# One level of Strassen's algorithm in the first product of a four-expert mixture layer

## The chip, the cores and the metric

The kernel runs on one core of one Trainium2 chip. The metric is the device time of one execution in microseconds (us). TensorE (PE) multiplies, VectorE (DVE), ScalarE (ACT) and GpSimd (POOL) work element by element, and SyncE (SP) issues the transfers. Each engine takes its instructions in the order in which the program lists them, and semaphores order the engines among each other.

## What is computed

```python
# attention on q, k, v in chunks of 64 tokens -> x [2304, 512]
a = x @ w_a; b = x @ w_b                  # [512, 1536] each
x = (a * b) @ w_out                       # [1536, 512]
p = domain_probs / (domain_probs.sum(-1, keepdims=True) + 1e-09)
for e in range(4):                        # w1 [4, 512, 1024], w2 [4, 1024, 512]
    h = np.maximum(x @ w1[e], 0.0)
    out += p[:, e:e + 1] * (h @ w2[e])
```

The change concerns the products `x @ w1[e]` and the order of everything in the loop over the experts.

## The kernel before

The 2304 tokens are 18 tiles of 128, in five blocks: block 0 has two tiles (256 tokens), blocks 1 to 4 have four (512 tokens). Activations lie with the features on the partitions and the tokens along the free dimension until the last product.

Every dense product is taken on float32r parts. An operand is split as hi, its rounding to float32r (a cast on ACT, `split_hi`, L84), and lo, the remainder (a subtraction, on POOL for the weights, L158). `mm3` (L305 to L312) issues three matmuls for each 128 rows of the contraction: hi·lo, hi·hi, lo·hi. Each matmul has its own weight load.

The first stage runs attention beside the first of 12 chunks of `w_a`, `w_b`, `w_out` (`moe1_steps`, `x2_steps`). For each chunk and block: the a products (12 matmuls), the b products (12), a copy of a on ACT (L336), the product a·b on DVE (L340), its split (hi on ACT, lo on POOL, L344); and one block later the 12 matmuls with `w_out`, whose results DVE adds to `xacc` (L374). In the last chunk each finished quarter of `xacc` is split on the spot into `yh` (ACT) and `yl` (POOL, L377): those are the inputs of the mixture.

The second stage (L523 to L532) walks 16 groups g of two chunks of 128 hidden features, and in each the five blocks. `emit_h` makes one chunk's hidden values of a block: 12 matmuls into one PSUM bank, `hh` by Relu on ACT (L392), `hl` by DVE from the same bank (L393). `emit_o`, one block behind, makes for each tile the 6 matmuls with w2 and one DVE instruction (L423) that scales by p and adds to `oacc`; the last group also stores. Two blocks' work is interleaved this way so that the hidden values are ready when their products come:

```python
for j in range(NB):
    for f in range(g * G2, g * G2 + G2):
        emit_h(f, j)
    if pend:
        emit_o(*pend)
    pend = (g, j)
```

Weights come in pieces of [128, 512] through three `raw` buffers (`load_w`, on SP, L109); a piece is loaded when the piece three before it has been split. Six `wh`/`wl` pairs hold the split pieces. PSUM is used as a ring of eight banks (`psum`, L75). The order of instructions on every engine is the order of the source (`manual_schedule`); the semaphores follow from the tiles.

Of the kernel before, what the change touches and what calls it, by code (L numbers as in the profile page):

```python
# [28 lines left out]
def fused_kernel(  # L29
# [104 lines left out]

    ready = {}

    def prep_begin(n, upto):
        for _ in range(n):
            if nxt["begin"] < min(upto, len(pieces)):
                key = pieces[nxt["begin"]]  # L140
                nxt["begin"] += 1
                r = raws.pop(key)
                ready[key] = from_f64(r) if key[0] == 0 else r

    def prep_end(n, upto):
        for _ in range(n):
            if nxt["prep"] < min(upto, len(pieces)):
# [3 lines left out]
                if key[0] == 1 and nxt["prep"] % 4 == 0:  # L151
                    pool, n_b = late["h"], 2
                else:
                    pool, n_b = w_p, 6
                hi = pool.tile([P, 512], F32R, tag="wh", name="wh", bufs=n_b)
                lo = pool.tile([P, 512], F32R, tag="wl", name="wl", bufs=n_b)
                split_hi(hi, r)
                nc.gpsimd.tensor_tensor(out=lo, in0=r, in1=hi.bitcast(F32), op=ALU.subtract)  # L158
                wts[key] = (hi, lo)
# [226 lines left out]
    def emit_h(f, j):
        n = blocks[j][1] * P
        ps = psum()
        mm3(ps, kparts(wts[1, f, 0], xh[j], xl[j]), n)
        hh = late["h"].tile([P, 512], F32R, tag="hh", name="hh", bufs=2 * G2)  # L390
        hl = late["h"].tile([P, 512], F32R, tag="hl", name="hl", bufs=2 * G2)
# [202 lines left out]
```

## Time and profile before

| | us |
|---|---|
| median of 3 runs (lowest, highest) | 1311.74 (1311.53, 1312.3) |
| span of the profiled execution | 1309.5 |
| busy in that span: PE, DVE, POOL, ACT | 1296.1, 619.2, 291.9, 279.8 |

The busy time of PE counts a matmul from its start to its end, and successive matmuls overlap, so a matmul's own duration is not what one more matmul costs; that is the distance from one start to the next. The second stage, from 519.4 us on, takes some 60% of the span.

### The profile page before, as it was taken

Reading aid. Unit: us, or ns where it says so; the run is one execution under the profiler, and the core shown is the slowest. Engines: PE = TensorE matmul, PEld = TensorE weight load, DVE = VectorE, ACT = ScalarE, POOL = GpSimd, SP = SyncE. Lnnn points to the kernel's source line nnn. Section 1 sums busy time; section 2 is a strip of 40 time slices with the busy share of each in tenths; the row PEclk is TensorE's granted clock in tenths of the full one; section 3 lists DMA queues with packets and bytes.
Section 4 is the critical chain, followed back from the end, with each engine's and each line's share of the span. In section 5 each row is a group of like instructions: output and inputs, shape, how many; then the busy total and the mean of one; then the engine's idle time right before and its main releaser. Section 6 shows DMA issues by size and latency. Waiting matters only on the chain.

```text
span 1309.5 us, 16332 instructions
## 1 busy us (share of the span) xinstructions
PE 1296.1 (99%) x6818; PEld 1083.4 (83%) x6820; DVE 619.2 (47%) x985; ACT 279.8 (21%) x517; POOL 291.9 (22%) x247
## 2 busy tenths in 40 slices
PE   8899999999999999999999999999999999999998
PEld 5788888888888888888888888888888888888887
DVE  7964555555655544344344344344344344344344
ACT  3544222222222225111111111111111111111110
POOL 4523333433433338210110110110110110110100
PEclk9999999999999999999999999999999999999999
DMA  8721111111111000100000000000000000000003
GB/s 273 221 89 33 40 41 35 47 49 49 49 37 45 25 25 25 33 20 22 25 18 23 25 19 23 25 18 24 25 18 23 25 18 24 25 17 24 1 24 121
DMA packets 25272, 55.60 MB, mean 42 GB/s; under 512 B 3184, under 2 KB 3184, under 8 KB 25200
## 3 DMA queue, kind: packets, MB, share of 16 engines
q1 hardware_dynamic: 25200, 54.58, 13.5%
q8 instruction: 53, 0.87, 0.3%
q14 instruction: 19, 0.16, 0.0%
HBM read 49.84 MB, written 4.72 MB: 42 GB/s over the span
## 4 chain that ended last, share of the span: by engine, by line
PE 94%; DVE 4%; issue 0%; ACT 0%; DMA 0%; POOL 0%; SPq 0%; DVEq 0%
PE ps L310 31%; PE ps L311 31%; PE ps L312 31%; PE ps L261 1%; DVE d L212 1%; DVE sm L223 0%; DVE mx L210 0%; DVE cv L116 0%; PE ps L196 0%; DVE xl L274 0%; DVE sm L224 0%; DMA kbd<-in_k_dram 0%; DVE cv L119 0%; DVE cv L122 0%; PE ps L233 0%
## 5 line engine op out<-in xcount | busy, mean ns | idle before, releaser
L423 DVE SCALAR_TENSOR_TENSOR oacc<-ps,pr,oacc 128x512 f32<-128x512 f32 x270 | 202.8, 751 | 129.4 <-PE ps L312 127.0
L393 DVE SCALAR_TENSOR_TENSOR hl<-ps,hh 128x512 fp32r<-128x512 f32 (+1 forms) x160 | 102.1, 638 | 329.9 <-ACT hh L392 329.9
L311 PE MATMUL ps<-yh,wh 128*128 128x512 f32 (+1 forms) x640 | 235.4, 368 | 0.0
L312 PE MATMUL ps<-yh,wl 128*128 128x512 f32 (+1 forms) x640 | 235.4, 368 | 0.0
L310 PE MATMUL ps<-yl,wh 128*128 128x512 f32 (+1 forms) x640 | 235.3, 368 | 0.0
L392 ACT ACTIVATE hh<-ps 128x512 fp32r<-128x512 f32 (+1 forms) x160 | 88.8, 555 | 655.2 <-PE ps L312 655.1
L310 PE MATMUL ps<-wl,hh 128*128 128x512 f32 x576 | 224.3, 389 | 0.0
L311 PE MATMUL ps<-wh,hh 128*128 128x512 f32 x576 | 224.2, 389 | 0.0
L312 PE MATMUL ps<-wh,hl 128*128 128x512 f32 x576 | 224.1, 389 | 0.0
L158 POOL TENSOR_TENSOR wl<-raw,wh 128x512 fp32r<-128x512 f32 x64 | 82.7, 1292 | 633.4 <-ACT wh L84 633.4
L310 PE MATMUL ps<-xl,wh 128*128 128x512 f32 (+1 forms) x488 | 179.7, 368 | 3.4 <-DVE xl L274 2.9
L311 PE MATMUL ps<-xh,wh 128*128 128x512 f32 (+1 forms) x488 | 178.1, 365 | 0.0
L312 PE MATMUL ps<-xh,wl 128*128 128x512 f32 (+1 forms) x488 | 178.0, 365 | 0.0
L310 PEld LDWEIGHTS ps<-yl,wh 128*128 128x128 f32 x640 | 120.6, 188 | 20.5
L311 PEld LDWEIGHTS ps<-yh,wh 128*128 128x128 f32 x640 | 120.6, 188 | 20.5
L312 PEld LDWEIGHTS ps<-yh,wl 128*128 128x128 f32 x640 | 120.6, 188 | 20.0
L374 DVE TENSOR_TENSOR xacc<-ps,xacc 128x512 f32<-128x512 f32 (+1 forms) x220 | 132.7, 634 | 2.4 <-PE ps L312 2.4
L340 DVE TENSOR_TENSOR asb<-ps,asb 128x512 f32<-128x512 f32 (+1 forms) x61 | 38.5, 630 | 197.0 <-PE ps L312 170.4
L312 PEld LDWEIGHTS ps<-wh,hl 128*128 128x128 f32 x576 | 108.1, 188 | 22.6
L310 PEld LDWEIGHTS ps<-wl,hh 128*128 128x128 f32 x576 | 108.2, 188 | 22.1
L311 PEld LDWEIGHTS ps<-wh,hh 128*128 128x128 f32 x576 | 108.2, 188 | 21.9
L344 POOL TENSOR_TENSOR gl<-asb,gh 128x512 fp32r<-128x512 f32 (+1 forms) x61 | 71.5, 1172 | 168.5 <-ACT gh L84 168.5
(55 smaller groups left out, 1297.5 us busy)
## 6 DMA issues: line engine op xcount, KB each, us to landing
raw<-in_w1p_dram SPq DMA_DIRECT2D x36, 512.0 KB, 3.5
raw<-in_w2p_dram SPq DMA_DIRECT2D x64, 256.0 KB, 2.6
q<-in_q_dram SPq DMA_DIRECT2D x18, 256.0 KB, 4.7
kbd<-in_k_dram SPq DMA_DIRECT2D x36, 128.0 KB, 4.5
v<-in_v_dram SPq DMA_DIRECT2D x18, 256.0 KB, 3.5
out_dram<-oacc SPq DMA_DIRECT2D x18, 256.0 KB, 2.0
pr<-in_probs_dram SPq DMA_DIRECT2D x1, 36.0 KB, 4.3
```

The costliest lines, as they stand in the source:

```text
L158: nc.gpsimd.tensor_tensor(out=lo, in0=r, in1=hi.bitcast(F32), op=ALU.subtract)
L212: nc.vector.tensor_tensor(out=d, in0=ps, in1=mx.to_broadcast([P, H, CH]), op=ALU.subtract)
L261: nc.tensor.matmul(out=ps[s, hp, CH * c : CH * c + CH], lhsT=vv[s, c, hp, :], rhs=aT[s, hp, CH * c : CH * c + CH], start=True, stop=True,)
L310: nc.tensor.matmul(out=ps[:, :n], lhsT=wh, rhs=al, start=(m == 0), stop=False)
L311: nc.tensor.matmul(out=ps[:, :n], lhsT=wh, rhs=ah, start=False, stop=False)
L312: nc.tensor.matmul(out=ps[:, :n], lhsT=wl, rhs=ah, start=False, stop=(m == last))
L340: nc.vector.tensor_tensor(out=g[:, :n], in0=st[1][:, :n], in1=g[:, :n], op=ALU.mult)
L344: nc.gpsimd.tensor_tensor(out=gl[:, :n], in0=g[:, :n], in1=gh[:, :n].bitcast(F32), op=ALU.subtract)
L374: nc.vector.tensor_tensor(out=ac, in0=ps[:, :n], in1=ac, op=ALU.add)
L392: nc.scalar.activation(out=hh[:, :n], in_=ps[:, :n], func=ACTF.Relu)
L393: nc.vector.scalar_tensor_tensor(out=hl[:, :n], in0=ps[:, :n], scalar=0.0, in1=hh[:, :n].bitcast(F32), op0=ALU.max, op1=ALU.subtract,)
L423: nc.vector.scalar_tensor_tensor(out=o, in0=ps, scalar=p1, in1=o, op0=ALU.mult, op1=ALU.add)
```

## The change

The hidden values of blocks 1 and 2, and of 3 and 4, are made in pairs. For a group g, w1 is a 2×2 matrix of blocks (features in halves of 256, hidden chunks two) and the two token blocks with the feature halves are another. Instead of eight block products, `emit_h_pair` takes seven, each of 6 matmuls (`half_mm`), in Winograd's form of Strassen's algorithm: of sums S1 to S4 of w1's quarters and sums T1 to T4 of the activations' quarters. The results are put together by DVE additions through three temporary tiles (`u2`, `u3`, `c22`, `c21`, `c12`, and `m1`, a copy by ACT); two of the products accumulate into a PSUM bank that has been read before.

S1 to S4 are made on POOL (`w1_sums`) in each group, and split like weights: a group now splits six pieces (four of w1 and its sums, two of w2) where it split four. T1 to T4 are made in place in `xacc` (`combos`) and with B11, B21 and B22 split into seven pairs of half tiles, for blocks 1 and 2 during the end of the first stage and for blocks 3 and 4 during the first token pass.

There are now two passes over all 16 groups: one with blocks 1, 2 and 0, one with blocks 3 and 4. Every weight is loaded and split twice, as pieces of [128, 1024]. Block 0 keeps 24 plain matmuls of 256 tokens a group (`emit_h0`). In the last chunk of the first stage the blocks run in the order 1, 2, 0, 3, 4, and only block 0 still makes `yh` and `yl` there. `o_tiles` takes two tiles at a time into two banks and runs directly after its own group's hidden values, no longer one block behind. On the host, w1's second chunk has its feature halves swapped.

```diff
-    NF2 = w2p.shape[0]
+    NG2 = w2p.shape[0]
+    NF2 = 2 * NG2
...
-    pieces += [(1, f, i) for f in range(NF2) for i in range(2)]
+    pieces += [(1, g, i) for _ in range(2) for g in range(NG2) for i in range(2)]
...
-                    r = raw_p.tile([P, 512], F32, tag="raw", name="raw")
-                nc.sync.dma_start(out=r, in_=(w1p, w2p)[key[0]][key[1], :, key[2], :])
-                raws[key] = r
+                    r = raw_p.tile([P, 1024], F32, tag="raw", name="raw2")
+                    s = slice(2 * key[2], 2 * key[2] + 2)
+                    nc.sync.dma_start(
+                        out=r, in_=w2p[key[1], :, s, :].rearrange("p a n -> p (a n)")
+                    )
+                raws.setdefault(key, []).append(r)
...
+    def split_w(r):
+        hi = w_p.tile([P, 512], F32R, tag="wh", name="wh")
+        lo = w_p.tile([P, 512], F32R, tag="wl", name="wl")
+        split_hi(hi, r)
+        nc.gpsimd.tensor_tensor(out=lo, in0=r, in1=hi.bitcast(F32), op=ALU.subtract)
+        return hi, lo
...
-                if f == NF1 - 1:
+                if f == NF1 - 1 and j == 0:
...
-            if f == NF1 - 1:
+            if f == NF1 - 1 and j == 0:
...
+    def combos(j1, j2, tags):
+        y1, y2 = acc[j1], acc[j2]
+        q = [y1[:, 0:2, :], y1[:, 2:4, :], y2[:, 0:2, :], y2[:, 2:4, :]]
+        parts = {}
+        def hi(name, i):
+            pool, tag = tags[name]
+            t = pool.tile([P, KD, 512], F32R, tag=tag, name=f"c{name}")
+            parts[name] = (t[:, 0:2, :], t[:, 2:4, :])
+            split_hi(parts[name][0], q[i])
+        def lo(name, i, eng):
+            h, l = parts[name]
+            eng.tensor_tensor(out=l, in0=q[i], in1=h.bitcast(F32), op=ALU.subtract)
+        def sub(o, a, b):
+            nc.vector.tensor_tensor(out=q[o], in0=q[a], in1=q[b], op=ALU.subtract)
+        def split(name, i, eng):
+            return [lambda: hi(name, i), lambda: lo(name, i, eng)]
+        v, g = nc.vector, nc.gpsimd
+        first = split("B11", 0, g) + split("B21", 1, g)
+        early = [lambda: sub(0, 2, 0), lambda: sub(2, 3, 2)] + split("T3", 2, v)
+        early += [lambda: sub(2, 3, 0)] + split("T2", 2, v) + [lambda: sub(1, 2, 1)]
+        rest = split("T1", 0, v) + split("T4", 1, g) + split("B22", 3, v)
+        return first, early, rest, parts
...
+    def w1_sums(r):
+        a11, a12, a22, a21 = (r[:, 256 * i : 256 * i + 256] for i in range(4))
+        s23 = cv_p.tile([P, 512], F32, tag="cv", name="s23")
+        s14 = cv_p.tile([P, 512], F32, tag="cv", name="s14")
+        s2, s3 = s23[:, :256], s23[:, 256:]
+        s1, s4 = s14[:, :256], s14[:, 256:]
+        tt = nc.gpsimd.tensor_tensor
+        tt(out=s1, in0=a21, in1=a22, op=ALU.add)
+        tt(out=s2, in0=s1, in1=a11, op=ALU.subtract)
+        tt(out=s3, in0=a11, in1=a21, op=ALU.subtract)
+        return s23, s14, lambda: tt(out=s4, in0=a12, in1=s2, op=ALU.subtract)
+    def w_steps(g):
+        w = ring[g] = {}
+        st = {}
+        def halves(t, a, b):
+            for i, name in enumerate((a, b)):
+                w[name] = tuple(x[:, 256 * i : 256 * i + 256] for x in t)
+        def s0():
+            st["r"] = raws[1, g, 0].pop(0)
+            halves(split_w(st["r"][:, :512]), "A11", "A12")
+        def s1():
+            st["s23"], st["s14"], st["s4"] = w1_sums(st["r"])
+            halves(split_w(st["s23"]), "S2", "S3")
+        def s2():
+            st["s4"]()
+            halves(split_w(st["s14"]), "S1", "S4")
+        def s3():
+            halves(split_w(st["r"][:, 512:]), "A22", "A21")
+            load_w()
+        def s4():
+            st["r2"] = raws[1, g, 1].pop(0)
+            w[0] = split_w(st["r2"][:, :512])
+        def s5():
+            w[1] = split_w(st["r2"][:, 512:])
+            load_w()
+        return [s0, s1, s2, s3, s4, s5]
...
+    def half_mm(ps, w, b, first=True):
+        for kk in range(2):
+            wh, wl = (x[:, kk * P : kk * P + P] for x in w)
+            bh, bl = (x[:, kk, :] for x in b)
+            for m, (x, y) in enumerate(((wh, bl), (wh, bh), (wl, bh))):
+                nc.tensor.matmul(
+                    out=ps,
+                    lhsT=x,
+                    rhs=y,
+                    start=first and kk == 0 and m == 0,
+                    stop=kk == 1 and m == 2,
+                    skip_group_check=not first,
...
+    def emit_h_pair(w, c, w2_steps):
+        pa, pb = psum(), psum()
+        half_mm(pa, w["A11"], c["B11"])
+        m1 = tmp(0, "m1")
+        nc.scalar.copy(out=m1, in_=pa)
+        w2_steps.pop(0)()
+        half_mm(pb, w["S2"], c["T2"])
+        u2 = tmp(1, "u2")
+        add(u2, pb, m1)
+        half_mm(pa, w["A12"], c["B21"], first=False)
+        low11 = relu_parts("11", pa)
+        pc = psum()
+        half_mm(pc, w["S3"], c["T3"])
+        w2_steps.pop(0)()
+        low11()
+        u3 = tmp(2, "u3")
+        add(u3, pc, u2)
+        pd = psum()
+        half_mm(pd, w["S1"], c["T1"])
+        c22 = tmp(0, "c22")
+        add(c22, pd, u3)
+        low22 = relu_parts("22", c22)
+        pe = psum()
+        half_mm(pe, w["A22"], c["T4"])
+        c21 = tmp(2, "c21")
+        add(c21, pe, u3, ALU.subtract)
+        low21 = relu_parts("21", c21)
+        low22()
+        half_mm(pd, w["S4"], c["B22"], first=False)
+        c12 = tmp(1, "c12")
+        add(c12, pd, u2)
+        low12 = relu_parts("12", c12)
+        low21()
+        low12()
...
+    def emit_h0(w):
+        n = blocks[0][1] * P
+        hh = cv_p.tile([P, 2, n], F32R, tag="sg", name="hh0", bufs=1)
+        hl = cv_p.tile([P, 2, n], F32R, tag="rd", name="hl0", bufs=1)
+        for f, names in enumerate((("A11", "A12"), ("A21", "A22"))):
+            ps = psum()
+            parts = []
+            for kk in range(KD):
+                wh, wl = (x[:, kk % 2 * P : kk % 2 * P + P] for x in w[names[kk // 2]])
+                parts.append((wh, wl, xh[0][:, kk, :], xl[0][:, kk, :]))
+            mm3(ps, parts, n)
...
+        def step(i):
+            ps = [psum(), psum()]
+            for f, (hh, hl) in enumerate((h1, h2)):
+                for k in range(2):
+                    s = slice((i + k) * P, (i + k) * P + P)
+                    wh, wl = w[f]
+                    for m, (x, y) in enumerate(((hh, wl), (hh, wh), (hl, wh))):
+                        nc.tensor.matmul(
+                            out=ps[k],
+                            lhsT=x[:, s],
+                            rhs=y,
+                            start=f == 0 and m == 0,
+                            stop=f == 1 and m == 2,
+                        )
+                    if f == 1:
+                        evict(ps[k], i + k)
+        for i in range(0, nt, 2):
+            yield lambda i=i: step(i)
...
+        XTAGS = [[f"x{c}{j}" for j in js for c in "hl"] for js in ((1, 2), (3, 4))]
         x2 = []
+        w_next = []
+        side = []
...
+            order = (1, 2, 0, 3, 4) if f == NF1 - 1 else range(NB)
+            for j in order:
+                n = blocks[j][1]
...
+                if f == NF1 - 1 and r == 3:
+                    side = c_early + c_rest
+                if f == NF1 - 1 and r == 2:
+                    tags = {n: (late["h"], n) for n in ("B11", "T2", "B21")}
+                    tags |= zip(("T3", "T1", "T4", "B22"), ((act, t) for t in XTAGS[0]))
+                    side, c_early, c_rest, parts = combos(1, 2, tags)
...
+                    if side and (i % 2 or r == 2):
+                        side.pop(0)()
...
+                    w_next = w_next or w_steps(0)
+                    if r < 3 or r == 4:
+                        w_next.pop(0)()
...
-        pend = None
-        for g in range(NF2 // G2):
-            for j in range(NB):
-                for f in range(g * G2, g * G2 + G2):
-                    emit_h(f, j)
-                if pend:
-                    emit_o(*pend)
-                pend = (g, j)
-                prep_w(4 if j == NB - 1 else 1, 3 * NF1 + 2 * G2 * (g + 2))
-        emit_o(*pend)
+        for step in side:
+            step()
+        for p, (j1, j2) in enumerate(((1, 2), (3, 4))):
+            for g in range(NG2):
+                w = ring[g]
+                end = p == 1 and g == NG2 - 1
+                assert len(w_next) == 2
+                if p == 0 and g == 0:
+                    emit_h0(w)
+                emit_h_pair(w, parts, w_next)
+                if not end:
+                    w_next = w_steps((g + 1) % NG2)
+                if p == 0 and g:
+                    emit_h0(w)
+                steps = list(o_tiles(g, w, j1, hs["11"], hs["21"]))
+                steps += o_tiles(g, w, j2, hs["12"], hs["22"])
+                if p == 0:
+                    h0 = [(hs["0"][0][:, f, :], hs["0"][1][:, f, :]) for f in range(2)]
+                    steps += o_tiles(g, w, 0, *h0)
+                if p == 0 and g == 0:
+                    tags = dict(zip(("B11", "T3", "T2", "B21"), ((act, t) for t in XTAGS[1])))
+                    tags |= {n: (late["h"], t) for n, t in zip(("T1", "T4", "B22"), ("B11", "T2", "B21"))}
+                    side, c_early, c_rest, parts_b = combos(3, 4, tags)
+                    side += c_early
+                if p == 0 and g == NG2 - 1:
+                    side = side + c_rest
+                for i, step in enumerate(steps):
+                    step()
+                    if len(w_next) > 2:
+                        w_next.pop(0)()
+                    if p == 0 and side and (i == 1 or g == NG2 - 1):
+                        for _ in range(len(side) if i == len(steps) - 1 else 2):
+                            side.pop(0)()
+            if p == 0:
+                parts = parts_b
```

## Rows read from the trace of the kernel before

**Rows 1.** The page's list of busy time by engine and two lines of its 40 equal slices of the span.
```profile
PE 1296.1 (99%) x6818; PEld 1083.4 (83%) x6820; DVE 619.2 (47%) x985; ACT 279.8 (21%) x517; POOL 291.9 (22%) x247
...
PE   8899999999999999999999999999999999999998
...
PEclk9999999999999999999999999999999999999999
```

**Rows 2.** The chain of work that ended last, by engine, from the page.
```profile
PE 94%; DVE 4%; issue 0%; ACT 0%; DMA 0%; POOL 0%; SPq 0%; DVEq 0%
```

**Rows 3.** Busy time by stretch: one group of the second stage, from its block 1 to the next group's, twice. Columns: stretch, length, busy time (and count) of PE, PEld, DVE, ACT, POOL, the granted clock, the DMA share, GB/s.
```profile
522.25:571.27 49.02, 49.02 (x230) 41.06 (x229) 19.58 (x28) 8.48 (x16) 10.66 (x9) 1.00 0.09 27
571.27:620.30 49.03, 49.03 (x229) 41.10 (x228) 19.90 (x28) 7.59 (x14) 5.17 (x4) 1.00 0.07 22
```

**Rows 4.** Timeline of PE at the change of stages: the wait of block 4's product with `w_out` (released by POOL), and the first and last of block 0's 24 matmuls of 256 columns with the next one of 512. Columns: start, duration, engine, line, operation.
```profile
515.97 0.39 PE L312 MATMUL ps<-gh,wl 128*128 128x512 f32 x1
516.53 0.50 PE L310 MATMUL ps<-gl,wh 128*128 128x512 f32 x1 [0.17 <-POOL gl L344]
...
519.38 0.28 PE L310 MATMUL ps<-yl,wh 128*128 128x256 f32 x1
...
522.13 0.28 PE L312 MATMUL ps<-yh,wl 128*128 128x256 f32 x1
522.25 0.40 PE L310 MATMUL ps<-yl,wh 128*128 128x512 f32 x1
```

**Rows 5.** Timeline of all engines in the second stage: the last matmul of a hidden chunk, what follows it on ACT and DVE, and a matmul with its weight load.
```profile
901.39 0.39 PE L312 MATMUL ps<-yh,wl 128*128 128x512 f32 x1
...
901.82 0.60 ACT L392 ACTIVATE hh<-ps 128x512 fp32r<-128x512 f32 x1 [2.12 <-PE ps L312]
...
902.08 0.19 PEld L310 LDWEIGHTS ps<-wl,hh 128*128 128x128 f32 x1
902.30 0.39 PE L310 MATMUL ps<-wl,hh 128*128 128x512 f32 x1
...
902.45 0.69 DVE L393 SCALAR_TENSOR_TENSOR hl<-ps,hh 128x512 fp32r<-128x512 f32 x1 [2.03 <-ACT hh L392]
```

**Rows 6.** Groups of instructions with shapes kept apart: operation, shapes, count, busy time, mean ns of one, idle time before them and its releaser. DVE, then POOL, then ACT.
```profile
L374 DVE TENSOR_TENSOR xacc<-ps,xacc 128x512 f32<-128x512 f32 x176 | 117.2, 688 | 2.4 <-PE ps L312 2.4
L374 DVE TENSOR_TENSOR xacc<-ps,xacc 128x256 f32<-128x256 f32 x44 | 15.5, 416 | 0.0
L393 DVE SCALAR_TENSOR_TENSOR hl<-ps,hh 128x512 fp32r<-128x512 f32 x128 | 88.6, 692 | 296.0 <-ACT hh L392 296.0
L393 DVE SCALAR_TENSOR_TENSOR hl<-ps,hh 128x256 fp32r<-128x256 f32 x32 | 13.6, 425 | 33.9 <-ACT hh L392 33.9
L423 DVE SCALAR_TENSOR_TENSOR oacc<-ps,pr,oacc 128x512 f32<-128x512 f32 x270 | 202.8, 751 | 129.4 <-PE ps L312 127.0
L158 POOL TENSOR_TENSOR wl<-raw,wh 128x512 fp32r<-128x512 f32 x64 | 82.7, 1292 | 633.4 <-ACT wh L84 633.4
L377 POOL TENSOR_TENSOR yl<-xacc,yh 128x512 fp32r<-128x512 f32 x16 | 20.2, 1305 | 0.0
L377 POOL TENSOR_TENSOR yl<-xacc,yh 128x256 fp32r<-128x256 f32 x4 | 2.8, 744 | 0.0
L84 ACT CAST wh<-raw 128x512 fp32r<-128x512 f32 x64 | 39.3, 614 | 0.0
L84 ACT CAST yh<-xacc 128x512 fp32r<-128x512 f32 x16 | 9.9, 622 | 1.2 <-DVE xacc L374 0.5
L84 ACT CAST yh<-xacc 128x256 fp32r<-128x256 f32 x4 | 1.3, 402 | 0.0
L336 ACT COPY asb<-ps 128x512 f32<-128x512 f32 x47 | 27.4, 582 | 52.1 <-PE ps L312 51.0 <-POOL yl L377 1.1
L392 ACT ACTIVATE hh<-ps 128x512 fp32r<-128x512 f32 x128 | 76.5, 598 | 544.1 <-PE ps L312 544.1
```

**Rows 7.** The chain of work that ended last, in order of time, at the change of stages: start, duration, what.
```profile
513.74 0.70 DVE asb L340
514.47 0.64 ACT gh L84
515.17 1.31 POOL gl L344
```

**Rows 8.** Timeline: a DVE instruction with one tensor, in SBUF, that came while POOL was busy, and DVE additions (one operand in PSUM) beside the same POOL instruction.
```profile
306.49 1.08 DVE L374 TENSOR_TENSOR xacc<-ps,xacc 128x256 f32<-128x256 f32 x3
...
306.98 1.30 POOL L344 TENSOR_TENSOR gl<-asb,gh 128x512 fp32r<-128x512 f32 x1 [0.95 <-ACT gh L84]
307.49 1.07 DVE L116 TENSOR_SCALAR cv<-raw 128x512 f32<-128x512 f32 x1
```

**Rows 9.** Durations by source line, lowest, median and highest in ns: L116 (one tensor, in SBUF), L122 (two tensors, both in SBUF), L374 and L423 (one in PSUM, one in SBUF).
```profile
L116 DVE TENSOR_SCALAR cv<-raw x36: 376/420/1308, 11.5 to 463.7; 128x512 f32<-128x512 f32 x36
...
L122 DVE SCALAR_TENSOR_TENSOR cv<-cv,sg x36: 691/694/694, 13.5 to 465.0; 128x512 uint32<-128x512 uint32 x36
...
L374 DVE TENSOR_TENSOR xacc<-ps,xacc x220: 415/692/693, 121.2 to 519.6; 128x512 f32<-128x512 f32 x88, 128x256 f32<-128x256 f32 x22
...
L423 DVE SCALAR_TENSOR_TENSOR oacc<-ps,pr,oacc x270: 750/751/752, 578.4 to 1305.8; 128x512 f32<-128x512 f32 x135
```

**Rows 10.** The page's list of transfers: issuing queue, count, KB each, median us from issue to landing.
```profile
raw<-in_w1p_dram SPq DMA_DIRECT2D x36, 512.0 KB, 3.5
raw<-in_w2p_dram SPq DMA_DIRECT2D x64, 256.0 KB, 2.6
...
out_dram<-oacc SPq DMA_DIRECT2D x18, 256.0 KB, 2.0
```

More of the change, by code (lines that the diff above doesn't have):

```diff
@@ L138, in prep_begin @@
         for _ in range(n):
-            if nxt["begin"] < min(upto, len(pieces)):
+            if nxt["begin"] < min(upto, 3 * NF1):
                 key = pieces[nxt["begin"]]
                 nxt["begin"] += 1
-                r = raws.pop(key)
-                ready[key] = from_f64(r) if key[0] == 0 else r
+                ready[key] = from_f64(raws[key].pop(0))
     def prep_end(n, upto):
         for _ in range(n):
-            if nxt["prep"] < min(upto, len(pieces)):
+            if nxt["prep"] < min(upto, 3 * NF1):
                 key = pieces[nxt["prep"]]
@@ L150, in prep_end @@
                 r = ready.pop(key)
[L151 to L159, printed above, removed]
+                wts[key] = split_w(r)
                 load_w()
@@ L382, in x2_steps @@
             yield lambda dd=dd: step(dd)
-    hs = {}
[L386 to L391, printed above, removed]
-        nc.scalar.activation(out=hh[:, :n], in_=ps[:, :n], func=ACTF.Relu)
-        nc.vector.scalar_tensor_tensor(
-            out=hl[:, :n],
-            in0=ps[:, :n],
-            scalar=0.0,
-            in1=hh[:, :n].bitcast(F32),
-            op0=ALU.max,
-            op1=ALU.subtract,
-        )
-        hs[f, j] = (hh, hl)
+    def combos(j1, j2, tags):
[20 more added lines that the diff above has]
+        return first, early, rest, parts
@@ new lines, in tmp, with relu_parts, low @@
+    def tmp(i, name):
+        return g_p.tile([P, 512], F32, tag=("asb", "gh", "gl")[i], name=name)
+    hs = {}
+    def relu_parts(name, src):
+        hh = late["h"].tile([P, 512], F32R, tag=f"hh{name}", name="hh")
+        hl = late["h"].tile([P, 512], F32R, tag=f"hl{name}", name="hl")
+        nc.scalar.activation(out=hh, in_=src, func=ACTF.Relu)
+        hs[name] = (hh, hl)
+        def low():
+            nc.vector.scalar_tensor_tensor(
+                out=hl, in0=src, scalar=0.0, in1=hh.bitcast(F32), op0=ALU.max, op1=ALU.subtract
+            )
+        return low
@@ new lines, in emit_h0 @@
+    def emit_h0(w):
[9 more added lines that the diff above has]
+            mm3(ps, parts, n)
+            nc.scalar.activation(out=hh[:, f, :], in_=ps[:, :n], func=ACTF.Relu)
+            nc.vector.scalar_tensor_tensor(
+                out=hl[:, f, :],
+                in0=ps[:, :n],
+                scalar=0.0,
+                in1=hh[:, f, :].bitcast(F32),
+                op0=ALU.max,
+                op1=ALU.subtract,
+            )
+        hs["0"] = hh, hl
@@ L403, in fused_kernel, with o_tiles, evict @@
     oacc = {}
-    def emit_o(g, j):
+    def o_tiles(g, w, j, h1, h2):
         t0, nt = blocks[j]
         e = g * G2 // FPE
-        if g == 0:
-            oacc[j] = act.tile([P, nt, DM], F32, tag=f"acc{j}", name=f"oacc{j}")
-        for i in range(nt):
-            s = slice(i * P, i * P + P)
-            ps = psum()
-            parts = []
-            for f in range(g * G2, g * G2 + G2):
-                hh, hl = hs[f, j]
-                wh, wl = wts[1, f, 1]
-                parts.append((hh[:, s], hl[:, s], wh, wl))
-            mm3(ps, parts, DM)
+        def evict(ps, i):
+            if g == 0 and i == 0:
+                oacc[j] = act.tile([P, nt, DM], F32, tag=f"acc{j}", name=f"oacc{j}")
@@ L425, in emit_o @@
                 )
-            if g == NF2 // G2 - 1:
+            if g == NG2 - 1:
                 nc.sync.dma_start(out=out[(t0 + i) * P : (t0 + i + 1) * P, :], in_=o)
-        for f in range(g * G2, g * G2 + G2):
-            hs.pop((f, j))
+        def step(i):
[11 more added lines that the diff above has]
+                            stop=f == 1 and m == 2,
+                        )
+                    if f == 1:
+                        evict(ps[k], i + k)
+        for i in range(0, nt, 2):
+            yield lambda i=i: step(i)
     def domain_probs():
@@ L518, in fused_kernel @@
             if f == 0:
                 early.close()
-                late["h"] = ctx.enter_context(tc.tile_pool(name="h", bufs=2))
+                late["h"] = ctx.enter_context(tc.tile_pool(name="h", bufs=1))
         for step in x2:
             step()
-        pend = None
-        for g in range(NF2 // G2):
-            for j in range(NB):
-                for f in range(g * G2, g * G2 + G2):
-                    emit_h(f, j)
-                if pend:
-                    emit_o(*pend)
-                pend = (g, j)
-                prep_w(4 if j == NB - 1 else 1, 3 * NF1 + 2 * G2 * (g + 2))
@@ L565 @@
     w1p = _np.stack([by_f(wa), by_f(wb), by_rows(wo)], axis=2).view(_np.int64)
-    w2p = _np.concatenate(
-        [
-            _np.stack([by_f(a), by_rows(b)], axis=2)
-            for a, b in zip(inputs["moe2_w1"], inputs["moe2_w2"])
-        ]
-    )
+    w2p = []
+    for a, b in zip(inputs["moe2_w1"], inputs["moe2_w2"]):
+        a, b = by_f(a), by_rows(b)
+        swapped = _np.concatenate([a[1::2, :, 2 * P :], a[1::2, :, : 2 * P]], axis=2)
+        w2p.append(_np.stack([a[::2], swapped, b[::2], b[1::2]], axis=2))
+    w2p = _np.concatenate(w2p)
     pr = inputs["moe2_domain_probs"]
```

11 lines of the change are left out of this document (6 added, 5 removed).

## The prediction

> **What bounds the kernel now.** I read the page's busy times first: PE is busy for 99% of the span and its granted clock stands in the top tenth in every slice, that is at the 2.4 GHz level [rows 1]. The chain that ended last says the same: 94% PE, 4% DVE [rows 2]. So time goes when matmuls go, unless PE then has to wait. DVE is busy 47%, POOL and ACT about 21%, so on average there is room for more work on them.
>
> The second thing to read is what a matmul costs. Its duration, 0.39 us, is not the price: starts are closer than that. A group of the second stage takes 49.025 us (the mean of two) [rows 3] and holds 204 matmuls of 512 columns (block products 96, products with w2 108) and 24 of 256. The latter are priced at the change of stages: 24 of them from 519.38 to 522.25, 0.1196 each [rows 4]. So (49.025 - 2.87) / 204 = 0.2262 us for one of 512 columns. There is no idle PE in these windows, the weight load (0.19) lies under the matmul before it, and the clock is 1.00. PE is the only bound of this stage.
>
> **What is removed.** Per group and pair of blocks, 8 × 6 = 48 matmuls become 7 × 6 = 42. 16 groups × 2 pairs × 6 = 192 matmuls × 0.2262 = 43.4 us. The w2 products (6 a tile and group), block 0's 24 a group, and the first stage keep their counts. The number of weight loads falls with the matmuls. The profiled execution's 1309.5 us span would become 1266.1; the median of the runs lies 2.2 us above that span, so 1311.7 becomes 1268.3 if PE never waits. The rest asks where it waits.
>
> **The engines' new load, per group.** Prices from rows 6. DVE in pass 2: 5 additions (PSUM with SBUF, like L374, 0.69), 4 lo parts (0.69), 8 scalings (0.75) = 12.2 us. POOL: 6 lo parts at 1.29 and 4 sums of 256 columns at 0.74 = 10.7. ACT: 6 casts at 0.61, 4 Relus at 0.60, one copy at 0.58 = 6.6. PE in pass 2 takes 90 × 0.2262 = 20.4, in pass 1 (block 0 too) 102 × 0.2262 + 2.9 = 26.0. All fit on average; order and latency remain.
>
> **The seven products of a pair.** A product takes 6 × 0.2262 = 1.36. From the last matmul's start to the reader's start is 0.43 (901.39 to 901.82), so a result is readable 0.20 after the next product begins; from Relu's end (902.42) to DVE is 0.03 [rows 5]. Take pass 2, time 0 at the first product. m1's copy runs 1.56 to 2.15, and the third product, which accumulates on the same bank, starts at 2.72: 0.57 to spare. DVE does u2 at 2.92, low11 at 4.91, u3 at 5.64, c22 from 7.00 to 7.69; the seventh product accumulates on c22's bank from 8.16: 0.47 to spare. Then DVE has no gap: c21 from 8.36, low22 9.05, c12 9.74, low21 10.43 to 11.12, low12 to 11.81. Behind c12 in the queue stands low21, though its own data were there at 9.7. The first w2 products start at 9.52; they need hh11, hl11 and hh21 first, and hl21 as the third matmul of the second half, at 9.52 + 8 × 0.2262 = 11.33, its weight load at 11.11. So hl21 is late by about 0.0 to 0.1. In pass 1 block 0's plain products (2.9 us) lie between, except in the first group, where they stand ahead of the pair. So 17 places. Bounds: 0, and 0.35 each (half a DVE instruction of 0.69, if one gets behind); 0 to 6 us. I take 0.06 each, 1.0 us, since the walk ends within a few hundredths of the need.
>
> The split pieces of the next group: ACT casts them right behind the last Relu (11.1), POOL works from 11.7 to about 21.1 and on w2's lo parts from 2.8 to 4.1 and 5.5 to 6.8 of the next group. The first product needs its part from 13.0, the sixth the last one at 21.1 - 20.4 = 0.7. Covered by 6 us and more. If POOL fell behind by that, every group would wait.
>
> **The change of stages.** This is the tight place: T1 to T4 are made in 26 us. Instructions of 1024 columns are not in the trace; going on along the line from 256 to 512 columns [rows 6] they are estimated at 1.23 on DVE, 1.06 on ACT, 2.4 on POOL. Time 0 at block 0's span in the last chunk; PE alone would end that span at 5.6, block 3's at 12.5, block 4's a and b at 17.95, block 3's w_out products at 20.7, block 4's at 23.4, block 0's plain ones at 26.3. POOL and ACT follow each other in program order: w1's sums and S2, S3 to 4.3, B11 lo to 6.7, B21 lo to 9.1, block 0's gl 9.85, S4's sum 10.6. ACT stands waiting for that sum with the copy of block 3's a behind it (to 11.8), then T3's cast (12.9), T3 lo on DVE (14.2), block 0's four additions with another subtraction among them (17.1), T2's cast behind the last yh (18.65), T2 lo (19.9), a subtraction (21.1), and only then block 4's a·b, possible since 18.15, at 21.8; its gh 22.45, gl 23.8. PE wants gl at 20.7: it waits 3.15 us. Today the same chain (DVE 513.74, ACT 514.47, POOL 515.17) makes PE wait 0.33 [rows 4, 7]. Net 2.8. What comes after (B22, block 0's plain products, the first pair) is ready by then in this walk.
>
> The other bound is a conflict of DVE with POOL. A DVE instruction with one tensor in SBUF came at 307.49 during a POOL subtraction (306.98 to 308.28) and took 1.07 instead of 0.42 [rows 8, 9]: it was held to the end of the other. Additions with one operand in PSUM ran beside the same subtraction unharmed, at most 693 ns in all 220; scalings at most 752 [rows 8, 9]. The new subtractions and lo parts of `combos` have both operands in SBUF. Their nearest kind is L122, 694 at most in 36 [rows 9], but none of these met a POOL instruction under way, so the rows leave it open. If these exclude each other with POOL, the same walk, alternating, brings block 4's gl at 27.2 and a further 0.6 before block 0's second chunk: 6.5 + 0.6 - 0.3 = 6.8.
>
> The Trainium skill (SBUF — State Buffer, section "SBUF: two separate sides") states that DVE and GpSimd share a port pair as an exclusive lock, and names DVE instructions with two SBUF inputs among those that take it against a GpSimd one that reads SBUF. By that rule the stage change costs 6.8 and the forecast would be 1276.1; the trace shows the hold for one tensor (1.07 against 0.42), and no run here shows it for two.
>
> Between 2.8 and 6.8 I take 4.0, nearer to the end that L122's rows support. Below zero is not excluded, since 16 casts and 16 POOL subtractions of yh and yl go [rows 6], but PE's wait there is only 0.33 now, so no more than that can be gained.
>
> **With one answer.** Transfers: w1 and w2 come twice, 64 × 512 KB in place of 64 × 256; pieces of 512 KB land in 3.5 us [rows 10] and are issued about a group (20 us) ahead. On SP the stores of blocks 0 to 2 stand behind a load's wait for a buffer; nobody waits for them. At the end two banks finish 0.68 apart in place of 1.36, so the last scaling (0.75) starts 0.07 later. The combinations of blocks 3 and 4 lie two a group behind the second step of the w2 products, where the eight banks give PE several us. Their cover gone, each would cost at most its own 1.2 to 2.4 us.
>
> **Sum.** 1309.5 - 43.4 + 4.0 + 1.0 = 1271.1 of span, and 2.2 around it: 1273.3 us.
>
> **Rivals.** (a) Nothing waits: 1268.3. For it: the spare times above; against: the stage change's queue order. (b) The exclusion holds, and hl21 is late by 0.2 to 0.35 in the 17 places: 1268.3 + 6.8 + 3 to 6 = 1278 to 1281. For it: the held instructions of rows 8. (c) DVE's in-order queue makes the first w2 products of pass 2 wait a whole DVE instruction or two, about 1 us in 16 groups and 4 at the change: 1268.3 + 16 + 4 = 1288. Against: the walk shows a near meeting. (d) Slower: POOL is held by every DVE instruction, additions and scalings too. A group of pass 2 then takes POOL 10.7 + DVE 12.2 = 22.9 against PE's 20.4 (16 × 2.5 = 40), one of pass 1 10.7 + 14.6 + 1.1 (combinations) = 26.4 against 26.0 (6). 1268.3 + 46 + 5 = 1319. It outweighs the gain from 1.36 us a group on. Against: the additions of rows 8 and POOL's L158, 1.29 on average beside 270 scalings. (e) The change doesn't take the matmuls away: the listed products are six matmuls each, seven times, so I see no room for it; 1311 at 1%.
>
> **Chances.** Forecast (1270 to 1278) 0.58; (a) 0.13; (b) and what lies up to 1284, 0.17; (c) 0.08; (d) 0.03; (e) 0.01. Without the page's rule (b) would have 0.12. The range takes in (a) and (b): 1267.5 to 1284. Faster or slower counts from 0.2% (2.6 us), which is about what a measurement of this kernel can tell from no change: faster 0.95, same 0.02, slower 0.03.
>
> **What would show it.** Right: 192 fewer PE records of 512 columns and starts still 0.226 apart; a group of pass 1 at 26.0 and of pass 2 at 20.4 to 20.6; one PE wait of 2 to 7 us, released by POOL's gl in the last chunk. For the exclusion: `combos` subtractions over 1.3 us, ending with a POOL end. Wrong: PE waits in every group of pass 2 with DVE's hl as releaser (c), POOL lo parts well over 1.3 us and PE weight loads waiting for POOL (d), or a granted clock below 1.00 in the second stage.

## The result, and the profile after

The changed kernel takes 1275.47 us (median of 4 runs, 1273.98 to 1276.15) against 1311.98 (1311.53 to 1312.3, 4 runs): a ratio of 0.972, 95% interval 0.9707 to 0.9734. The forecast was 1273.3. The profiled execution's span is 1273.8 us. In two of the experiments below one execution ran at a low granted clock throughout (1567.45 us at 0.753 with the filling matmuls, 1436.53 us at 0.849 with the rearrangement alone), and the medians leave these two out. Line numbers below are those of the changed kernel (L318 and L320 are the first and last matmul of `mm3`, L344 the copy of a, L348 the product a·b, L352 gl, L90 every cast, L149 the lo parts of weights, L382 the additions to `xacc`, L408 and L411 the lo parts and subtractions of `combos`, L433 to L436 POOL's sums, L479 the matmuls of `half_mm`, L500 and L507 the lo parts and additions of a pair, L582 the scalings, L595 the w2 products).

Busy time by engine and the granted clock, from the page; they answer to [rows 1]:

```profile
PE 1253.6 (98%) x6626; PEld 1048.0 (82%) x6628; DVE 731.5 (57%) x1161; ACT 378.2 (30%) x675; POOL 550.9 (43%) x493
...
PEclk9999999999999999899999999999999999999999
```

There are 192 PE records fewer (6818 to 6626), as counted. One slice of the clock is no longer full. Busy time by stretch shows where; the columns are those of [rows 3], and the last row here is one group of pass 2, from its first product to the next group's:

```profile
510.00:515.00 5.00, 5.00 (x24) 4.14 (x23) 4.47 (x7) 2.40 (x6) 4.35 (x4) 1.00 0.00 0
515.00:520.00 5.00, 1.73 (x8) 1.11 (x6) 3.85 (x4) 2.93 (x5) 1.75 (x3) 1.00 0.00 0
520.00:525.00 5.00, 3.10 (x7) 2.48 (x8) 3.93 (x7) 2.64 (x4) 4.70 (x3) 0.54 0.00 0
525.00:530.00 5.00, 5.00 (x30) 4.46 (x29) 3.49 (x5) 0.38 (x1) 0.42 (x1) 0.78 0.31 105
...
550.00:900.00 350.00, 350.00 (x1691) 295.99 (x1691) 194.93 (x288) 99.87 (x179) 149.27 (x136) 1.00 0.13 42
...
1106.72:1127.11 20.39, 20.39 (x91) 16.89 (x90) 11.62 (x18) 6.38 (x11) 10.54 (x11) 1.00 0.17 51
```

A group of pass 2 takes 20.39, which is 90 × 0.2266: PE never stands. The whole loss lies between 515 and 530. PE's timeline there (it answers to [rows 4]), with the first matmul of block 0's span ahead of it:

```profile
495.88 0.28 PE L318 MATMUL ps<-xl,wh 128*128 128x256 f32 x1
...
516.34 0.39 PE L320 MATMUL ps<-gh,wl 128*128 128x512 f32 x1
521.90 0.79 PE L318 MATMUL ps<-gl,wh 128*128 128x512 f32 x1 [5.17 <-POOL gl L352]
522.49 0.63 PE L319 MATMUL ps<-gh,wh 128*128 128x512 f32 x1
522.92 0.63 PE L320 MATMUL ps<-gh,wl 128*128 128x512 f32 x1
...
527.18 0.30 PE L318 MATMUL ps<-yl,wh 128*128 128x256 f32 x1
```

Block 4's first w_out matmul could have started at 516.57 and starts at 521.90: 5.33 us. The twelve matmuls from there on take 5.28 us, 0.43 apart, where twelve at 0.226 take 2.71: the granted clock was 0.54 in that stretch, so most of them ran at the 1.2 GHz level, after PE had stood still. That is 2.57 more. Minus today's 0.33 [rows 4] the change of stages costs 7.6, and 1309.5 - 43.4 + 7.6 = 1273.7 against the measured span of 1273.8. The sum closes to 0.1 us.

The chain that makes gl late, on DVE, POOL and ACT (one timeline each):

```profile
504.01 2.19 DVE L411 TENSOR_TENSOR xacc<-xacc,xacc 128x1024 f32<-128x1024 f32 x1
506.24 1.65 DVE L411 TENSOR_TENSOR xacc<-xacc 128x1024 f32<-128x1024 f32 x1
...
512.40 1.65 DVE L411 TENSOR_TENSOR xacc<-xacc,xacc 128x1024 f32<-128x1024 f32 x1
...
516.15 1.69 DVE L408 TENSOR_TENSOR cT<-xacc,cT 128x1024 fp32r<-128x1024 f32 x1 [1.43 <-ACT cT L90]
517.76 1.21 DVE L411 TENSOR_TENSOR xacc<-xacc,xacc 128x1024 f32<-128x1024 f32 x1
518.90 0.68 DVE L348 TENSOR_TENSOR asb<-ps,asb 128x512 f32<-128x512 f32 x1
```

```profile
505.08 1.72 POOL L352 TENSOR_TENSOR gl<-asb,gh 128x256 fp32r<-128x256 f32 x1
506.76 1.72 POOL L436 TENSOR_TENSOR s<-raw,s 128x256 f32<-128x256 f32 x1
...
520.30 1.54 POOL L352 TENSOR_TENSOR gl<-asb,gh 128x512 fp32r<-128x512 f32 x1 [3.55 <-ACT gh L90]
```

```profile
508.51 0.62 ACT L90 CAST wh<-s 128x512 fp32r<-128x512 f32 x1 [6.37 <-POOL s L436]
509.04 0.58 ACT L344 COPY asb<-ps 128x512 f32<-128x512 f32 x1
...
516.02 0.58 ACT L344 COPY asb<-ps 128x512 f32<-128x512 f32 x1
```

Three things are to be seen. Block 4's a·b (DVE, 518.90) stands behind T2's lo part and a subtraction, though its matmuls were done by 514; the copy of its a on ACT (516.02) also comes two us after them. ACT waits 6.37 us for S4's sum with the copy of block 3's a right behind it. And DVE subtractions of 1024 columns, 1.21 when alone, last 1.65 to 2.19, while POOL instructions of 256 columns last 1.72 where they take 0.74 [rows 6].

### The profile page after: what moved, and what is told of

Its sections match the earlier page's. It is cut to its first block, busy times and chain, and to the rows that moved or that the text cites. A ratio compares the mean times of both kernels' runs of the same rounds, so it can differ in the third digit from the quotient of the medians.

```text
span 1273.8 us, 16939 instructions
## 1 busy us (share of the span) xinstructions
PE 1253.6 (98%) x6626; PEld 1048.0 (82%) x6628; DVE 731.5 (57%) x1161; ACT 378.2 (30%) x675; POOL 550.9 (43%) x493
## 4 chain that ended last, share of the span: by engine, by line
PE 92%; DVE 5%; POOL 1%; issue 1%; ACT 1%; DMA 0%; SPq 0%; DVEq 0%; POOLq 0%
PE ps L595 31%; PE ps L479 24%; PE ps L318 12%; PE ps L319 12%; PE ps L320 12%; PE ps L269 1%; DVE d L220 1%; DVE sm L231 1%; DVE mx L218 1%; DVE xl L282 0%; DVE cv L126 0%; DVE sm L232 0%; PE ps L204 0%; POOL cB L408 0%; DMA kbd<-in_k_dram 0%
## 5 line engine op out<-in xcount | busy, mean ns | idle before, releaser
L149 POOL TENSOR_TENSOR wl<-raw,wh 128x512 fp32r<-128x512 f32 x128 | 166.3, 1299 | 340.0 <-ACT wh L90 340.0
L582 DVE SCALAR_TENSOR_TENSOR oacc<-ps,pr,oacc 128x512 f32<-128x512 f32 x270 | 192.5, 750 | 141.4 <-PE ps L595 141.4
L595 PE MATMUL ps<-wl,hh 128*128 128x512 f32 x576 | 224.3, 389 | 0.0
L595 PE MATMUL ps<-wh,hh 128*128 128x512 f32 x576 | 224.2, 389 | 0.0
L595 PE MATMUL ps<-wh,hl 128*128 128x512 f32 x576 | 224.1, 389 | 0.0
L318 PE MATMUL ps<-xl,wh 128*128 128x512 f32 (+1 forms) x488 | 179.7, 368 | 2.3 <-DVE xl L282 1.8
L320 PE MATMUL ps<-xh,wl 128*128 128x512 f32 (+1 forms) x488 | 178.0, 365 | 0.0
L479 PE MATMUL ps<-cT,wh 128*128 128x512 f32 x512 | 157.6, 389 | 0.0
L348 DVE TENSOR_TENSOR asb<-ps,asb 128x512 f32<-128x512 f32 (+1 forms) x61 | 38.4, 630 | 191.4 <-PE ps L320 158.5
L352 POOL TENSOR_TENSOR gl<-asb,gh 128x512 fp32r<-128x512 f32 (+1 forms) x61 | 73.2, 1200 | 171.9 <-ACT gh L90 171.9
L382 DVE TENSOR_TENSOR xacc<-ps,xacc 128x512 f32<-128x512 f32 (+1 forms) x220 | 132.3, 633 | 4.0 <-PE ps L320 4.0
L595 PEld LDWEIGHTS ps<-wh,hl 128*128 128x128 f32 x576 | 108.1, 188 | 22.6
L595 PEld LDWEIGHTS ps<-wl,hh 128*128 128x128 f32 x576 | 108.2, 188 | 22.1
L595 PEld LDWEIGHTS ps<-wh,hh 128*128 128x128 f32 x576 | 108.2, 188 | 21.8
L479 PE MATMUL ps<-cB,wh 128*128 128x512 f32 x384 | 118.2, 389 | 0.0
L479 PEld LDWEIGHTS ps<-cT,wh 128*128 128x128 f32 x512 | 96.1, 188 | 20.0
L318 PEld LDWEIGHTS ps<-xl,wh 128*128 128x128 f32 x488 | 92.0, 188 | 18.5 <-DVE xl L282 2.6
L320 PEld LDWEIGHTS ps<-xh,wl 128*128 128x128 f32 x488 | 92.0, 188 | 14.9
L319 PEld LDWEIGHTS ps<-xh,wh 128*128 128x128 f32 x488 | 92.1, 189 | 14.4
L149 POOL TENSOR_TENSOR wl<-s,wh 128x512 fp32r<-128x512 f32 x64 | 83.2, 1299 | 47.2 <-ACT wh L90 47.2
L479 PE MATMUL ps<-cT,wl 128*128 128x512 f32 x256 | 99.6, 389 | 0.0
```

Source lines behind the costliest of these rows:

```text
L318: nc.tensor.matmul(out=ps[:, :n], lhsT=wh, rhs=al, start=(m == 0), stop=False)
L319: nc.tensor.matmul(out=ps[:, :n], lhsT=wh, rhs=ah, start=False, stop=False)
L320: nc.tensor.matmul(out=ps[:, :n], lhsT=wl, rhs=ah, start=False, stop=(m == last))
L348: nc.vector.tensor_tensor(out=g[:, :n], in0=st[1][:, :n], in1=g[:, :n], op=ALU.mult)
L352: nc.gpsimd.tensor_tensor(out=gl[:, :n], in0=g[:, :n], in1=gh[:, :n].bitcast(F32), op=ALU.subtract)
L382: nc.vector.tensor_tensor(out=ac, in0=ps[:, :n], in1=ac, op=ALU.add)
```

## The experiments

**Order.** Block 0's plain products go ahead of block 4's w_out products; the rest of `combos` is listed behind block 4's a·b; A22 and A21 are split earlier.

```diff
-                    if side and (i % 2 or r == 2):
+                    when = {2: 1, 3: i in (1, 3, 5, 7, 11), 4: 2 * (i > 8)}
+                    for _ in range(when.get(r, 0) if side else 0):
                         side.pop(0)()
+                    if f == NF1 - 1 and r == 4 and i == 4:
+                        w_next.pop(0)()
...
-                    if r < 3 or r == 4:
+                    if r < 3:
                         w_next.pop(0)()
...
+        emit_h0(ring[0])
         for step in x2:
             step()
...
-                if p == 0 and g == 0:
-                    emit_h0(w)
```

> Order of the change of stages altered: block 0's plain products go ahead of block 4's w_out products, the remaining combinations stand behind block 4's a*b in DVE's and ACT's queues, the split of A22 and A21 comes before it. Nothing is left out. Theory (place in the queues): block 4's gl is ready when PE wants it; the wait of 5.3 us shrinks to under 1 us, the granted clock stays at 1.00, the twelve matmuls behind take 2.7 in place of 5.3; 1267.5 to 1269 us. Rival (the sum of DVE and POOL work, which exclude each other, is what is late, wherever it stands): a wait of 3 to 5 us remains or comes back a few us later at the first pair's sums; 1272 to 1275.5.

Measured: 1268.66 us, ratio 0.9669 (0.9656 to 0.9682). PE's wait, from its timeline, and the two stretches that hold it:

```profile
520.21 0.50 PE L318 MATMUL ps<-gl,wh 128*128 128x512 f32 x1 [0.67 <-POOL gl L352]
```

```profile
510.00:520.00 10.00, 9.54 (x54) 8.20 (x52) 9.30 (x13) 5.93 (x11) 9.35 (x8) 1.00 0.09 20
520.00:530.00 10.00, 9.79 (x43) 8.13 (x44) 10.00 (x13) 4.76 (x8) 5.56 (x4) 1.00 0.08 32
```

0.67 us is left (0.83 by the distance of starts, as the 5.33 above is counted) and the clock stays at 1.00. DVE is busy for all of 520 to 530 and PE, past that wait, does not notice: the same work, held in the same way, fits when it stands behind what PE waits for. The place in the queues decided. This version beats both kernels and meets the time worked out for no waiting at all (1268.3).

**The clock.** 24 matmuls that nobody reads fill the wait.

```diff
+        keep_warm(24)
         for step in x2:
             step()
```

> 24 matmuls on constants, never read, are put where PE waits for block 4's gl (5.2 us of work). Theory (the slow matmuls behind the wait come from the granted clock, which fell because PE was idle): the wait is filled, the clock stays at 1.00, the twelve matmuls take 2.7 in place of 5.3; 1272.9 us. Rival (they are slow because of their operands or of DVE and POOL at work then): 1275.5 us, still 0.43 us apart.

Measured: 1273.42 us, ratio 0.9708 (0.9694 to 0.9721). PE's timeline and, behind it, two stretches of the same run, with the first 50 us of the changed kernel as a third fence:

```profile
517.96 5.42 PE L97 MATMUL ps<-const-bfloat16-1.0 128*128 128x512 bf16 x24
523.28 0.50 PE L318 MATMUL ps<-gl,wh 128*128 128x512 f32 x1
...
526.15 0.28 PE L318 MATMUL ps<-yl,wh 128*128 128x256 f32 x1
```

```profile
0.00:50.00 50.00, 43.09 (x498) 30.54 (x498) 37.58 (x68) 20.23 (x36) 23.05 (x29) 0.93 0.88 259
...
520.00:525.00 5.00, 5.00 (x23) 2.75 (x22) 5.00 (x8) 3.04 (x4) 3.31 (x2) 1.00 0.00 0
```

```profile
0.00:50.00 50.00, 41.14 (x506) 29.97 (x509) 38.84 (x70) 19.99 (x36) 24.16 (x30) 1.00 0.82 259
```

The twelve matmuls take 2.87 in place of 5.28, so their slowness came from PE standing still and not from their operands, nor from DVE and POOL, which are at work in this stretch too. From the end of block 3's products to block 0's first plain one it is 8.2 us against 10.6, 2.4 less. The medians differ by 2.1; the first 50 us, which neither change touches, differ in granted clock between these two profiles (0.93 and 1.00) and so block 3's products end 1.4 us later here (517.96 against 516.57).

**The eighth product.** A product that is never read comes back in every pair.

```diff
+        half_mm(psum(), w["S4"], c["B22"])
         c12 = tmp(1, "c12")
```

> Every pair takes an eighth product of six matmuls into a bank that is never read (S4 with B22 again); the output is the same. Theory (PE alone bounds both passes): 32 x 6 matmuls at 0.2262 come back, 1275.5 + 43.4 = 1318.9 us. Rival (PE waits somewhere in each group, for sums or lo parts, and the extra product fills part of it): under 1312.

Measured: 1318.45 us, 43.0 more than the changed kernel; 192 matmuls at 0.224. PE is the only bound of both passes.

**The rearrangement alone.** Two passes, doubled loads and the new order, but eight plain products.

```diff
     def emit_h_pair(w, c, w2_steps):
-        pa, pb = psum(), psum()
...
+        for i in (1, 2):
+            for f in (1, 2):
+                ps = psum()
+                half_mm(ps, w[f"A{f}1"], c[f"B1{i}"])
+                half_mm(ps, w[f"A{f}2"], c[f"B2{i}"], first=False)
+                low = relu_parts(f"{f}{i}", ps)
+                if i == 1:
+                    w2_steps.pop(0)()
+                low()
```

> The two token passes, the doubled loads, the pairs of tiles and block 0's place stay; the pairs are made by the eight plain products, without the sums S and T, so that nothing is put together by DVE. Theory (the gain is the seventh product alone and the rearrangement costs nothing, and the wait at the change of stages comes from the sums): the time of the kernel before, 1311 to 1313 us, PE wait at the change under 1 us. Rival (the rearrangement gains or costs by itself): outside 1309 to 1315.

Measured: 1311.88 us, ratio 1.0002 (0.9993 to 1.0012). PE's wait at the change of stages is what it was in the kernel before:

```profile
516.88 0.50 PE L318 MATMUL ps<-gl,wh 128*128 128x512 f32 x1 [0.16 <-POOL gl L352]
```

The second pass over the weights, 16.8 MB more of loads and the new order of tiles together cost nothing that shows; the sums make both the gain and the wait.

**The near meeting.** In the changed kernel hl21 is ready just in time. DVE, PE and PE's weight loads, pass 2:

```profile
1116.44 0.69 DVE L507 TENSOR_TENSOR c<-u,ps 128x512 f32<-128x512 f32 x1
1117.05 0.69 DVE L500 SCALAR_TENSOR_TENSOR hl<-c,hh 128x512 fp32r<-128x512 f32 x1
```

```profile
1117.83 0.39 PE L595 MATMUL ps<-wh,hh 128*128 128x512 f32 x1
1118.06 0.39 PE L595 MATMUL ps<-wh,hl 128*128 128x512 f32 x1
```

```profile
1117.83 0.19 PEld L595 LDWEIGHTS ps<-wh,hl 128*128 128x128 f32 x1
```

hl21 ends at 1117.74. Its weight load runs under the matmul before its own, from 1117.83: 0.09 to spare.

```diff
-        low21()
         low12()
+        low21()
```

> hl12 is made before hl21 on DVE; nothing else is altered. In the profile of the changed kernel hl21 ends 0.09 us before its weight load starts in pass 2. Theory (the walk of the seven products holds to a tenth of a us, and PE does not go round a weight load that waits): hl21 comes 1.45 us later, 1.36 too late, in the 16 groups of pass 2 and the first of pass 1, covered elsewhere by block 0's plain products: 17 x 1.36 = 23, 1298.5 us. Rival (there is more spare time than the profile shows): 1275.5 us.

Measured: 1332.38 us, 56.9 more, where 23 was expected. PE's waits in total, then timelines of PE, DVE and POOL in one group:

```profile
PE ps L595 <- DVE hl L500: 34.6, 17, 2.4
```

```profile
1173.47 0.39 PE L595 MATMUL ps<-wh,hh 128*128 128x512 f32 x1
1175.95 0.76 PE L595 MATMUL ps<-wh,hl 128*128 128x512 f32 x1 [2.08 <-DVE hl L500]
```

```profile
1173.53 2.36 DVE L500 SCALAR_TENSOR_TENSOR hl<-c,hh 128x512 fp32r<-128x512 f32 x2 [0.76 <-ACT hh L496]
```

```profile
1174.09 1.26 POOL L149 TENSOR_TENSOR wl<-raw,wh 128x512 fp32r<-128x512 f32 x1 [4.91 <-ACT wh L90]
```

Behind the wait, two stretches (columns of [rows 3]), one in this group and one in another:

```profile
1176.00:1179.00 3.00, 3.00 (x7) 2.40 (x8) 1.50 (x2) 0.62 (x1) 2.19 (x4) 0.50 0.00 0
...
985.50:989.00 3.50, 3.50 (x16) 2.87 (x17) 1.73 (x3) 0.62 (x1) 2.69 (x4) 1.00 0.00 0
```

The 17 places are as foretold, so the walk's few hundredths were real. The price was not: two lo parts of 0.69 take 2.36, since the second, both operands in SBUF, runs into POOL's subtraction (1174.09 to 1175.35) and ends half a us behind it, about 1.0 later than alone. And behind eleven of the waits some seven matmuls are 0.43 apart, at the lower clock level. By the distance of starts the 17 waits come to 37.4 us, and the matmuls behind them take 19.7 more than at 0.2266: 57.1, the whole loss. Behind the other six the clock stays at 1.00 (985.50), though five of them are as long, 2.25 us; the traces do not show what decides.

**The hold, by itself.** Two additions with both operands in SBUF behind every w2 step of pass 2.

```diff
+                    if p == 1:
+                        scr = cv_p.tile([P, 512], F32, tag="sg", name="scr", bufs=1)
+                        wh, wl = (x.bitcast(F32) for x in w[0])
+                        for _ in range(2):
+                            nc.vector.tensor_tensor(out=scr, in0=wh, in1=wl, op=ALU.add)
```

> In pass 2 two DVE additions of 512 columns with both operands in SBUF, never read, stand behind each of the four w2 steps of a group (128 in all), where POOL makes the sums and lo parts of the next group. Theory (a DVE instruction with two SBUF operands and a POOL instruction exclude each other): those that meet a POOL instruction last up to 0.69 + 1.29 us, or POOL's last up to 0.69 longer, while the scalings, one operand in PSUM, stay at 0.75; PE does not notice, 1275 to 1277 us. Rival (the long subtractions at the change of stages have another reason): all 128 at 0.69, POOL at 1.29 and 0.74.

Measured: 1284.31 us. Durations by source line, lowest, median, highest in ns (the added instructions, one of POOL's sums, the scalings):

```profile
L749 DVE TENSOR_TENSOR scr<-wh,wl x128: 675/1114/1717, 957.3 to 1280.4; 128x512 f32<-128x512 f32 x128
...
L435 POOL TENSOR_TENSOR s<-raw x32: 731/959/1720, 498.1 to 1252.3; 128x256 f32<-128x256 f32 x32
...
L582 DVE SCALAR_TENSOR_TENSOR oacc<-ps,pr,oacc x270: 734/751/752, 568.5 to 1279.0; 128x512 f32<-128x512 f32 x135
```

The 32 sums are from both passes. In pass 2 alone, first in the changed kernel, then here, with PE's waits in pass 2 here:

```profile
L435 POOL TENSOR_TENSOR s<-raw x17: 736/738/1722, 907.8 to 1243.6; 128x256 f32<-128x256 f32 x17
...
L435 POOL TENSOR_TENSOR s<-raw x15: 1179/1185/1189, 958.9 to 1252.3; 128x256 f32<-128x256 f32 x15
...
PE ps L479 <- DVE c L507: 3.8, 15, 0.5
```

The hold is shown, and both sides bear it: DVE's additions have a median of 1.11 in place of 0.69, this sum of POOL's takes 1.18 to 1.19 in all 15 groups in place of 0.74, and the scalings with one operand in PSUM stay at 0.75. "PE does not notice" was wrong: eight at a mean of 1.14 add 9.1 us to DVE's 12.2 a group, more than the group's 20.4, and the seventh product then waits for c22 (15 times, 0.5 us at most; by the distance of starts 7.7 of the 8.8 us lost). I had priced them at 0.69, against the theory that they were to test.

**Two smaller changes of the order.** First, group 0's sums and their splits are each listed one span earlier, ahead of block 0's span; the altered order above leaves them where they were.

```diff
-                    if r < 3 or r == 4:
+                    for _ in range((2, 1, 0, 0, 1)[r]):
                         w_next.pop(0)()
```

> Group 0's sums S1 to S4 and their splits are made two spans earlier, before block 0's span of the last chunk begins; the order of all else is that of the changed kernel. Theory (ACT's wait for S4's sum, with the copy of block 3's a behind it, and POOL's holds pass down the chain to block 4's gl): copy and product of block 3 come 2 us earlier and so does gl; PE's wait falls from 5.3 to about 3 us, the time to 1273 us, or 1270.5 if the clock then stays at 1.00. Rival (the chain subtraction, cast, lo part on DVE and ACT sets the time by itself): the wait stays at 5 us, 1275.5 us.

Measured: 1271.46 us, ratio 0.9689 (0.9676 to 0.9702). ACT and PE:

```profile
504.75 0.59 ACT L344 COPY asb<-ps 128x512 f32<-128x512 f32 x1 [3.82 <-PE ps L320]
```

```profile
519.39 0.67 PE L318 MATMUL ps<-gl,wh 128*128 128x512 f32 x1 [2.39 <-POOL gl L352]
```

The copy of block 3's a now waits for PE, at 504.75 in place of 509.04, and the wait for gl is 2.55 (519.39 - 516.84). The sums' place was about one half of the delay; T2 and a subtraction still stand ahead of block 4's a·b. The clock still fell, for the first eight or so of the twelve matmuls.

Second, of the altered order only block 0's products ahead of block 4's (the last two pieces of the first diff, and A22 and A21 split at the same early step).

> Of the altered order only one piece: block 0's plain products stand ahead of block 4's w_out products (with A22 and A21 split before them), the combinations stay where the changed kernel has them. Theory (gl is as late as before, 2.9 us of the wait are filled): PE waits 2.0 to 2.5 us there, less than 1 for A21's lo part; the clock stays at 1.00 or falls for a part; 1270 to 1272.5 us. Rival (DVE, behind by its queue, makes the first pair wait for what it did not have to before): over 1273 us.

Measured: 1273.05 us, ratio 0.9704 (0.9691 to 0.9718), above the theory's range and just inside the rival's; the waits decide:

```profile
519.38 0.39 PE L320 MATMUL ps<-yh,wl 128*128 128x256 f32 x1 [0.61 <-POOL wl L149]
...
523.33 0.80 PE L318 MATMUL ps<-gl,wh 128*128 128x512 f32 x1 [2.49 <-POOL gl L352]
```

```profile
518.11 2.30 DVE L411 TENSOR_TENSOR xacc<-xacc,xacc 128x1024 f32<-128x1024 f32 x1
```

```profile
517.55 1.77 POOL L149 TENSOR_TENSOR wl<-raw,wh 128x512 fp32r<-128x512 f32 x1 [0.45 <-ACT wh L90]
```

One wait of 2.65 for gl (520.68 to 523.33), one of 0.8 for A21's lo part, about half the twelve matmuls at the lower clock, and the first pair does not wait: the rival's mechanism is not there, and the filling works. But gl is not as late as before, it is 1.1 us later: 6.39 behind the end of block 3's products (523.33 - 516.94) against 5.33, since the subtraction ahead of block 4's a·b now meets the early lo part of A21 and takes 2.30 in place of 1.21.

From this run to the altered order only the place of the combinations differs. There gl comes 3.71 behind (520.21 - 516.50), 2.68 earlier than here and 1.62 earlier than in the changed kernel, and the time is 4.4 us lower than here: T2 and the subtraction in front of block 4's a·b were a good part of the rest of the delay.

## Why the prediction was right

The gain: 192 matmuls at 0.2262, the distance of starts and not the duration of 0.39, were priced at 43.4; the eighth product puts back 43.0. Priced by the duration they would have been 74.7.

The rearrangement at zero: right, 1.0002.

The seven products: the walk put hl21's end 0.0 to 0.1 behind the need. Measured it is 0.09 ahead of it; the 1.0 us taken for 17 places is 0 in the changed kernel. The spare time is as thin as that: one exchanged instruction cost 57 us.

The change of stages: the mechanism was right, the term was mis-sized. Forecast 4.0 between 2.8 and 6.8; measured 7.6, outside both bounds. Of it, PE's wait is 5.33, inside the walk's ends (3.15 without the hold, 6.5 with it). With time 0 at 495.88, PE wants gl at 20.7, as walked, and gl ends at 26.0 (23.8 without the hold, 27.2 with it). The hold was there, and I had leaned to the end that L122's rows supported. Those rows could not speak: none of the 36 had met a POOL instruction. The other 2.57 is a term that the sum did not have: the wait has a price behind it, since the granted clock falls. The two misses, 3.6 too little here and 1.0 too much for hl21, pull against each other, and that is luck: in the span they leave 2.6, 1271.1 against 1273.8, and in the medians 1273.3 against 1275.5.

The Trainium skill's rule on the shared port pair (SBUF — State Buffer, "SBUF: two separate sides") counts two SBUF inputs among what takes the lock; the trace agrees, with 1.65 to 2.19 us for subtractions that take 1.21 alone, and 1.72 for POOL instructions that take 0.74.

Rival (a), nothing waits, is what the altered order reaches (1268.66). Rivals (c) and (d) are refuted: no wait in pass 2, and POOL's lo parts stay at 1.30 beside the scalings. Rival (b) was half right: the hold, without a wait for hl21.

## What to carry to other kernels

Where one engine bounds, price removed work by the distance of starts and then look for the one place where the new helper work stands ahead, in an in-order queue, of something the bound engine wants; moving it behind that, with block 0's products put ahead, gave 6.8 us here for no change in the work (2.4 with the products alone, 4.4 more with the moving). A mean load of 57% says nothing about such a place. And when the trace has no pair of instructions that met, its unharmed durations are no evidence that they don't hold each other up.
